# Turning k and q on VectorE instead of TensorE in an attention-and-MLP kernel, with another split of the weight conversion and another fixed order

## The chip, the cores and the metric

The kernel runs on one core of a Trainium2 chip. A core has a matmul engine (TensorE, PE in the profile, with its weight loads shown as PEld), a vector engine (VectorE, DVE), an activation engine (ScalarE, ACT), a general engine (GpSimd, POOL) and a queue engine that issues most transfers (SyncE, SP). Each engine works through its own list of instructions in order and waits on semaphores for the others. The metric is device time in microseconds (us) of one execution; lower is better.

## The reference

Two blocks follow each other. The first is attention with random features (8 batches, 8 heads, 576 positions, 64 values a head, 128 features); the second takes the result as a matrix of 8 x 576 rows of 512, adds the real part of its two-dimensional Fourier transform, and applies a normalised two-layer MLP with 2048 hidden values.

```python
q_s, k_s = q * scale, k * scale
def phi(x):                                   # x: b h s d
    proj = einsum('bhsd,md->bhsm', x, omega)
    h = proj - sum(x * x, -1) / 2
    return exp(h - max(h, -1)) / sqrt(m)
q_p, k_p = phi(q_s), phi(k_s)
kv  = einsum('bhsm,bhsd->bhmd', k_p, v);  z = sum(k_p, axis=2)
out = (q_p @ kv) / (q_p @ z + 1e-06)
x   = out.transpose(0, 2, 1, 3).reshape(8, 576, 512)
u   = x + real(fft(fft(x, axis=1), axis=2))
un  = (u - mean(u)) / sqrt(var(u) + 1e-06)
y   = u + maximum(un @ w_ch1, 0) @ w_ch2
```

q, k, v and omega come as float32, the two weight matrices as float64.

## The kernel before

The work has two parts.

**The first part** holds the attention, the Fourier mixing, the conversion of the weights to float32, the MLP of the first 512 rows ("plain"), and preparations for the second part. Attention goes over 32 pairs of heads (`attn(n)`, L573), three pairs in flight. For a pair, the 128 partitions hold 64 blocks of nine positions for each of two heads, so k and q are nine slices of 128 x 64 each.

1. `loads` (L369) brings k and q of a pair into one buffer `kq` with one transfer each (L376, L379) on SP; there are two such buffers. `load_v` (L381) brings v (L384).
2. `transposed` (L495) turns k and q on PE: nine 128 x 128 transposes against an identity (L512), each of them two slices. They land in PSUM, and `evicted` (L516) copies them to `kqT` on ACT or DVE (L526, L528).
3. `pairs_of` (L592) multiplies the turned slices by omega (L606), in three groups of 4, 1 and 4 transposes. The first six pairs use matmuls with 64 x 128 weights ("wide"), the others four quarter-sized ones.
4. `softmax` (L542) takes the maximum over the features on DVE (L549) and the exponential on ACT (L566), 18 exponentials of 128 x 128 a pair.
5. The features of k are multiplied with v (L640); `keep` (L649) copies the sums to `kv` on DVE or ACT (L654, L656).
6. The features of q are turned on PE, again nine transposes and three evictions, which also bring the positions into the order of the Fourier step (`qeT`).
7. Numerator and denominator (L687, L695), then the division on DVE (L704, L705, L716) or with ACT (L712).

`mix` (L728) does the Fourier step for a batch after its four pairs: sums and differences ("folds", L743 to L779, DVE or POOL), matmuls against tables (L799 to L860), combinations (L898, L901 on DVE) and sums into x (L910, L911, DVE or POOL), which go to memory as `us`.

`narrow` (L427) turns a 128 x 512 piece of float64 weights into float32, 32 pieces in all, each brought by one 512 KB transfer (L469) into one of four `slab` buffers. A step on ACT or POOL scales the high words (L439, L437); DVE takes the sign bit (L442), shifts the bits and joins the sign (L444), masks the exponent (L447) and scales the low words by it (L449); a last add, on POOL or DVE, joins both (L455). When all are converted, `w2_parts` (L1119) forms sums of the second weights (L1138, DVE or POOL) in the slabs and stores them (L1161, L1163), and `block_norms` (L1097) prepares the first block of the second part (norms L966, factors L1113).

**The second part** (from L1252) does the MLP of the other rows in eight blocks of 512 with products of sums; weights come back from memory through 13 `wl` buffers (L1335). `weight_sums` (L1183) makes the sums of the first weights, the first quarter of them in a tile of its own.

**The order.** All steps are generators that yield a `Step`: the engine (or a choice of engines), an estimated duration, what it waits for, what buffers and PSUM banks it takes and gives. `Listing.run` (L184) keeps a clock per engine and picks one step after the other; the order in which it picks them is the order of every engine's list. In the first part a string `PICKS` (L63) fixes each choice, one character for a step: which waiting stream goes on, and whether its second-best engine is taken. The banks are chosen by the clock. The second part has no string and goes by the clock and a bias in each step. SP's transfers stand in the same order, and one that waits for a buffer holds back all behind it.

Of the kernel before, what the change touches and what calls it, by code (L numbers as in the profile page):

```python
# [39 lines left out]
class Clock(NamedTuple):  # L40
# [16 lines left out]
DIGITS = "0123456789abcdefghijklmnopqrstuvwxyzABCDEFGHIJKLMNOPQRSTUVWXYZ!#$%&()*+,"  # L57
# [4 lines left out]

PICKS = (  # L63
    "40e0f03eafdaegebg3NbcbeefdcOdeccfgdb37ghj0gjj7hlP79Kj7ik97i8S7efhjffeHldfPiehdjfdOShgihidaKOdbRhciff"
    "ecgOfeejdfdPdeeedgSfdffdOfd8Kiii88jhd8jP8b99i8e8jcddghjgheiifcecdciieicgPgdef9cdghbkededfgchbggb79ij"
    "8hi7hjaPN97aj9gfffeg8eif8hcej1jccc7ehidbhffLiQObfbeG766gggfcbjahj9Ofghhjj8dgkkgT6jghff8de6dUjfhbgegh"
    "MefRafjUf8jgciSjeckkhjakkaeikggjlioklnRSgodonON7l7l6nnj9icadc97cibPJIej788a7edhclhkmjjagVijihkkfpVim"
    "oklilTTillaghlhnmVjkmpjkhhnmkimlgglmbjpjjg9d9alafhhdjlacdTback0j766k7lh4g89Gck6gkki77gij5ijhgj6dimni"
    "3ndjgi6Kc4jldlaikbkaijbhf75dcjlmUVUDGci45jciekajkkUk5kihoUeaeobaiodlenMSdonbiiljjcWjjkboijjkkhgMfkik"
    "hiflkmOFF99nol5m8jT7naabda89Rbj97ecdl8cjilegiPkQb4acahg57ebbgabgdjkdTkk6eceebb5f9dg4RGce486ggg6egfhh"  # L70
    "fg4g9egf5cbdRgfhhhcgjhggejigibbmHnbedijj6Neb7biihi9bgihckaffPa8cijdhbdghbaeibdefffacjiciQSfi9JJ75ih5"
    "jgjI699ajfg6g7fgefd65bO6Kalkkgd5jgjikagfldliPJpeoaeeOPQNejadgilgicljiSSFe65k56kl5Hk7j67S9lilk9gliih6"
    "ffUgec4fg4dbgg7fedaif5gfbheefilddddddeQhg9kbfncggRcfkkafkag6ngb65p5Hopoj4bhoaXbelli68bjjl5b7dlhiQRhi"
    "lflhpkgiWomjknmmmUimnjbjhnJjkm5akPFgedccff6Wf7idUVhi8Th3fogbqp8fgmkeidjna7ckeXYghmnmffnjeo79q6547oa4"
    "nlkpd7aceonnc8bViVicilbhmjim8fh7Snn8l5mkkPjgfRhfhihg8ghfbS4kjf83j4lllb79jei8mnUblfnmmiolpilOki9Mh5l5"
    "pmnaOm79jjVmkbblekFiji9a9kffjgjikhiihfgjafhgfigh4g50fff0ba5fdh9dghda77hgfdcbg8eO988jcehefibjjkellPcc"
    "fcdhgcihPgcffba2f82b3c98cbcdcd6a299efgddb9KGQQbefLa9ecf74gg9867RgP9idg8kgOhePP7be6ff2e5cc8fbMgdaf8f8"
# [44 lines left out]
class Listing:  # L122
# [4 lines left out]
    def __init__(self, buffers):  # L127
# [4 lines left out]
        self.moved = 0.0  # L132
        self.mode = "whole"
        self.banks = [0.0] * 8
        self.got = None

    def banks_at(self, n, t):

# [142 lines left out]
def kernel(  # L281
# [29 lines left out]

    NS = 3
    NV = 3
    NKQ = 2
    NE = 7
    NWIDE = 6

# [1252 lines left out]
```

## Time and profile before

| | |
|---|---|
| median of 3 runs | 1179.16 us (1177.43 to 1181.72) |
| span of the profiled execution | 1180.9 us |
| first part, up to the first matmul of L1252 | 423.7 us |
| second part | 757.3 us |
| busy over the span: PE, DVE, ACT, POOL | 1164.9, 722.6, 452.4, 412.9 us |
| busy in the first part: PE, DVE, ACT, POOL | 412.7, 340.8, 282.3, 174.5 us |
| transfers in the first part | 181 GB/s, share of the 16 transfer engines 0.60 |

The profile gives the span of its own execution, which is within the spread of the timed runs; a separate time of that execution is not listed. A line of groups reads: source line, engine, operation, output <- input, shapes, count | busy us, mean ns | idle time of the engine ahead of it and who ended it. The chain is the work that ended last, followed back step by step. Matmuls are pipelined and their durations overlap, so PE's busy time says less than the chain's pieces, in which each matmul is counted from the end of the one before.

### The profile page before, as it was taken

To read this page: it belongs to the slowest core of one execution; us is meant where nothing else is said; L and a number is where in the kernel's file an instruction comes from. 1 tells how busy PE (TensorE), PEld (TensorE's weight loads), DVE (VectorE), ACT (ScalarE), POOL (GpSimd) and SP (SyncE) were. 2 spreads that over 40 slices of the span, in tenths; PEclk is the share of its full clock that TensorE was granted. 3 is DMA by queue.
4 is the path that set the end of the run, shared out by engine and by line. 5 is a ranking of instruction groups with operands and counts; after the bars stand their busy time and mean duration, and the time that the engine had idled before them with its cause. 6 is when DMAs were issued, how large, how long until landed. Compare 5 with 4: busy or idle time off the path is not lost.

```text
span 1180.9 us, 31428 instructions
## 1 busy us (share of the span) xinstructions
PE 1164.9 (99%) x12549; PEld 1044.6 (88%) x12549; DVE 722.6 (61%) x1552; ACT 452.4 (38%) x1513; POOL 412.9 (35%) x489
## 2 busy tenths in 40 slices
PE   8999999999999999999999999999999999999998
PEld 7878888779787878998998998998999899899898
DVE  7989999976677642762662572473374275266255
ACT  7987888866343212222222222222222222222211
POOL 2443544455462124214314304223322421431421
PEclk9999999999999999999999999999999999999999
DMA  8855756666662260861771582384295095177155
GB/s 238 245 165 173 244 174 180 200 197 178 188 203 91 88 224 10 291 194 52 240 242 64 174 286 85 118 293 134 63 304 179 10 301 193 44 245 236 63 169 189
DMA packets 144705, 205.67 MB, mean 174 GB/s; under 512 B 49072, under 2 KB 58544, under 8 KB 144560
## 3 DMA queue, kind: packets, MB, share of 16 engines
q1 hardware_dynamic: 144064, 203.41, 53.9%
q8 instruction: 99, 1.62, 0.6%
q14 instruction: 46, 0.38, 0.1%
q10 hardware_dynamic: 496, 0.26, 0.1%
HBM read 171.90 MB, written 35.91 MB: 176 GB/s over the span
## 4 chain that ended last, share of the span: by engine, by line
PE 90%; DVE 4%; DMA 3%; ACT 1%; issue 1%; SPq 1%; DVEq 0%; ACTq 0%
PE banks L1252 33%; PE banks L1432 30%; PE banks L1045 5%; PE banks L606 4%; PE banks L1068 4%; PE banks L512 4%; PE banks L640 2%; PE banks L687 2%; DMA kq<-in_q_dram 2%; PE banks L985 2%; PE banks L849 1%; PE banks L799 1%; DVE nmx L549 1%; PE banks L809 1%; DMA kq<-in_k_dram 1%
## 5 line engine op out<-in xcount | busy, mean ns | idle before, releaser
L1238 DVE CUSTOM_DVE_ANT_0 hid<-banks,s 128x256 f32<-128x256 f32 x192 | 79.6, 423 | 255.4 <-PE banks L1252 250.5
L1432 PE MATMUL banks<-wl,sums 128*128 128x128 f32 x1792 | 217.3, 275 | 0.0
L1432 PEld LDWEIGHTS banks<-wl,sums 128*128 128x128 f32 x1792 | 208.8, 192 | 0.4
L566 ACT ACTIVATE e<-banks,nmx 128x128 f32<-128x128 f32 x576 | 164.7, 428 | 24.5 <-DVE nmx L549 24.0
L1266 ACT ACTIVATE s<-banks 128x256 f32<-128x256 f32 x192 | 73.7, 384 | 261.1 <-PE banks L1252 261.1
L1252 PE MATMUL banks<-unT,w 128*128 128x256 f32 x704 | 167.5, 379 | 0.0
L1252 PEld LDWEIGHTS banks<-unT,w 128*128 128x128 f32 x704 | 132.7, 190 | 17.9 <-issue 0.5
L1407 ACT ACTIVATE s<-banks 128x128 f32<-128x128 f32 x168 | 46.6, 278 | 242.3 <-PE banks L1432 195.7
L1252 PE MATMUL banks<-tt,w1s 128*128 128x256 f32 x512 | 126.2, 379 | 0.0
L1319 POOL TENSOR_TENSOR hs<-hid 128x256 f32<-128x256 f32 x64 | 46.4, 725 | 207.9 <-DVE hid L1238 178.9
L1252 PEld LDWEIGHTS banks<-tt,w1s 128*128 128x128 f32 x512 | 97.3, 190 | 13.2
L1412 DVE TENSOR_TENSOR part<-banks,s 128x128 f32<-128x128 f32 x168 | 48.8, 291 | 88.6 <-PE banks L1432 88.4
L549 DVE TENSOR_REDUCE nmx<-banks 128x8 f32<-128x1024 f32 (+1 forms) x96 | 89.3, 951 | 21.6 <-PE banks L606 16.8
L1432 PE MATMUL banks<-wl,hid 128*128 128x128 f32 x768 | 97.6, 275 | 0.0
L1432 PEld LDWEIGHTS banks<-wl,hid 128*128 128x128 f32 x768 | 93.5, 192 | 1.2
L1319 POOL TENSOR_TENSOR hs<-hid,hs 128x256 f32<-128x256 f32 x64 | 46.6, 728 | 119.8 <-issue 94.9
L606 PE MATMUL banks<-om,kqT 64*64 64x128 f32 (+1 forms) x2088 | 80.2, 278 | 2.2 <-ACT kv L656 0.9
L1252 PE MATMUL banks<-unT,w1s 128*128 128x256 f32 x320 | 80.7, 379 | 0.0
L606 PEld LDWEIGHTS banks<-om,kqT 64*64 64x64 f32 (+1 forms) x2088 | 65.4, 140 | 13.8 <-issue 4.4
L979 POOL TENSOR_TENSOR rstd<-rstd,mhalf 128x1 f32<-128x1 f32 x36 | 24.8, 689 | 149.6 <-DVE rstd L977 148.6
L1432 PE MATMUL banks<-wl,hs 128*128 128x128 f32 x576 | 74.9, 275 | 0.4 <-DVE part L1412 0.4
L1432 PEld LDWEIGHTS banks<-wl,hs 128*128 128x128 f32 x576 | 70.0, 192 | 0.9 <-DVE part L1412 0.6
(128 smaller groups left out, 1951.6 us busy)
## 6 DMA issues: line engine op xcount, KB each, us to landing
wl<-w2l SPq DMA_DIRECT2D x392, 256.0 KB, 3.6
raw<-in_moe_w_ch_dram SPq DMA_DIRECT2D x32, 512.0 KB, 5.0
kq<-in_k_dram SPq DMA_DIRECT2D x32, 288.0 KB, 4.4
kq<-in_q_dram SPq DMA_DIRECT2D x32, 288.0 KB, 4.8
vd<-in_v_dram SPq DMA_DIRECT2D x32, 288.0 KB, 4.9
u<-us SPq DMA_DIRECT2D x36, 256.0 KB, 3.9
ur<-us SPq DMA_DIRECT2D x36, 256.0 KB, 3.8
out_dram<-ur SPq DMA_DIRECT2D x34, 256.0 KB, 2.4
```

The lines of the kernel that those rows point to most:

```text
L512: nc.tensor.transpose(ps[:, (j - j0) * 128 : (j - j0 + 1) * 128], src(j), ident[:])
L549: nc.vector.tensor_reduce(nmx[:, :, 0:num], pps[:, :, 0 : MF * num].rearrange("p b (c m) -> p b c m", m=MF), axis=AX.X, op=ALU.max, negate ...
L566: nc.scalar.activation(out=e[:, c + (i if num == 1 else 0), :], in_=pps[:, i, MF * c : MF * c + MF], func=AF.Exp, bias=nmx[:, i, c : c + 1],)
L606: nc.tensor.matmul(pps[cols, c, MF * m : MF * m + MF], lhsT=kqT[rows, j, cols], rhs=om2[rows, :],)
L1045: nc.tensor.matmul(hp[:, 0:TP], lhsT=w1[:, dc, 128 * fc : 128 * fc + 128], rhs=unTs[key][:, dc, :], start=(dc == 0), stop=(dc == NDC - 1),)
L1068: nc.tensor.matmul(yp[:, 0:DM], lhsT=hs[fc][:, 128 * i : 128 * i + 128], rhs=w2[:, fc, :], start=(fc == 0), stop=(fc == NFC - 1),)
L1238: nc.vector._custom_dve(TENSOR_ADD_SAT, out=o, in0=ps, in1=sb, s0=FMAX, s1=0.0)
L1252: nc.tensor.matmul(ps[:, 0:HT], lhsT=left(dc), rhs=right(dc), start=start and dc == 0, stop=(dc == D2 - 1), skip_group_check=True,)
L1266: nc.scalar.activation(out=s[:], in_=ps[:, 0:HT], func=AF.Copy)
L1319: nc.gpsimd.tensor_tensor(out=o, in0=l, in1=r, op=op)
L1412: nc.vector.tensor_tensor(out=part[:, t, 128 * m : 128 * m + 128], in0=ps[:, 0:128], in1=saved[with_][:], op=ALU.add,)
L1432: nc.tensor.matmul(ps[:, 0:128], lhsT=left[:, f], rhs=wls[j, i, n][:, f], start=start and f == 0, stop=(f == 3), skip_group_check=True,)
```

## The change

**k and q.** Each of them is brought separately into a buffer `kq` of 128 partitions x 1120 values; three buffers. For each of the two heads, 32 rows of 18 positions are loaded twice, into two groups of 32 partitions, the second time 32 values later ("shifted"). In a row of the buffer every second run of 32 values then belongs to one half of the head's 64 values, so that a DVE transpose of 32 x 32 blocks, over the runs at even places, gives a tile whose partitions are the 64 values of each head and whose columns are the positions. For k this is one instruction of 576 values, written at every second place; for q it is one of 512 and one of 64. The PE transposes of k and q and their evictions are gone. All projections are quarter-sized. The positions are grouped otherwise than before, so v is loaded in four pieces to match, the product with v keeps two partial sums, and `keep` adds them with a DVE reduction. The features of q take ten transposes (2, 4 and 4) instead of nine.

**The weights.** ACT scales the low words by a power of two and converts them (32 passes more); the two DVE passes over the exponent and the low words are gone; the last add is always on POOL.

**The sums of w2** and their stores: each store is its own step, and the next sums wait for the stores that read their tile only.

**Buffers.** `wl` has 12 instead of 13; the sums of the first weights for the first quarter, and part of those for the second, go into three `kq` buffers, so `kq` stays allocated in the second part.

**The order.** `PICKS` has two characters for a step: the stream, and the engine with the bank. On SP the last of the 32 weight transfers stands after the loads of 30 pairs (before: 25), the first part has 548 transfers (before: 260), and over the first part folds, sums into x and sums of w2 change between DVE and POOL: 24 sums of w2 go from POOL to DVE, and 16 of the last fold steps (L772), 6 of the first (L743) and 6 pairs of sums into x (L910, L911) go the other way, each net.

```diff
-    NKQ = 2
+    NKQ = 3
+    NTURN = 3
+    NQE = 2
-    NWIDE = 6
+    XR = 2 * R * D - D // 2
-    NWL, NSUM = 13, 3
+    NWL, NSUM = 12, 3
...
     def loads():
-            yield Step(SP, 0.37, 3.0, take=("kq",), makes=("k", n), kb=288)
-            kq = ld.tile([P, 2 * R, D], F32, name="kq", tag="kq")
-            nc.sync.dma_start(kq[:, 0:R, :], k[b, h].rearrange(rows, r=R))
-            yield Step(SP, 0.47, 3.6, makes=("kq", n), kb=288, bias=-2.98)
-            nc.sync.dma_start(kq[:, R : 2 * R, :], q[b, h].rearrange(rows, r=R))
+            for name, src in (("k", k), ("q", q)):
+                yield Step(SP, 1.35, 3.0, take=("kq",), makes=(name, n), kb=560, ...)
+                t = ld.tile([P, XR], F32, name="kq", tag="kq")
+                for i in range(2):
+                    rows = src[b, 2 * pr + i].rearrange("(x r) d -> x (r d)", r=2 * R)
+                    for dh in range(2):
+                        p0 = D * i + 32 * dh
+                        nc.sync.dma_start(t[p0 : p0 + 32, :], rows[:, 32 * dh : 32 * dh + XR])
...
     def load_v(n):
+        for i, h, r0, r1, c0 in ((0, 0, 0, 5, 0), (0, 1, 5, 9, 0), (1, 0, 0, 4, 5), (1, 1, 4, 9, 4)):
+            nc.sync.dma_start(vds[n % NV][D * h : D * h + D, c0 : c0 + r1 - r0, 0:D], ...)
...
     def narrow(i, dst, raw):
+        def rounding():
+            yield Step(ACT, 0.57, after=(("raw", i),), makes=("low", i), bias=1.11)
+            nc.scalar.activation(out=lo, in_=lo, func=AF.Copy, scale=2.0**-29)
+        yield Fork(rounding())
...
-        nc.vector.tensor_scalar(sign[:], bits, 0xFF800000, None, op0=ALU.bitwise_and)
-        nc.vector.scalar_tensor_tensor(
-            lof, lo, 2.0**-52, sign[:].bitcast(F32), op0=ALU.mult, op1=ALU.mult
-        )
-        step = Step({POOL: 1.25, DVE: 0.61}, makes=("w", i), give=("slab",), ...)
-        eng.tensor_tensor(out=dst, in0=dst, in1=lof, op=ALU.add)
+        yield Step(POOL, 1.25, after=(("low", i),), makes=("w", i), give=("slab",), ...)
+        nc.gpsimd.tensor_tensor(out=bits, in0=bits, in1=lo, op=ALU.add)
...
+    def turn(name, n):
+        yield Step(DVE, 0.7, after=((name, n),), take=("kT",), give=("kq",), makes=(name + "T", n))
+        t = att.tile([128, 2 * R * 32], F32, name="kT", tag="kT", bufs=NTURN)
+        raw = kqs.pop((name, n))[:].rearrange("p (r d) -> p r d", d=32)[:, ::2, :]
+        raw = raw.rearrange("p (s c) y -> p s c y", s=2)
+        if name == "k":
+            nc.vector.transpose(t[:].rearrange("p (c x s) -> p s c x", c=R, s=2), raw)
+        else:
+            nc.vector.transpose(
+                t[:, 0 : 64 * (R - 1)].rearrange("p (s x w) -> p s w x", s=2, x=32), raw[:, :, R - 1 : 0 : -1]
+            )
+            nc.vector.transpose(t[:, 64 * (R - 1) :].rearrange("p (s x) -> p s x", s=2), raw[:, :, 0])
+        return t
...
     def attn(n):
-        kqT = yield from transposed(...)
+        kT = yield from turn("k", n)
+        def turn_q():
+            qTs.append((yield from turn("q", n)))
+        yield Fork(turn_q())
...
+        yield from projected(lambda i, h, m: of_k(i, (NC + 1) * h + m), NC, 0, 1, after=(("kT", n), "om2"))
+        yield from projected(
+            lambda i, h, m: of_k(i, NC) if i == h else first_of_q(i), 1, 2, after=(("qT", n),), give=("kT",)
+        )
+        yield from projected(lambda i, h, m: of_q(i, m, h), NC, 3, 4, give=("kT",))
...
         def keep():
-            step = Step({DVE: 0.2, ACT: 0.16}, take=("kv",), give=(kvb,), makes=("kv", n))
+            yield Step(DVE, 0.34, take=("kv",), give=(kvb,), makes=("kv", n))
+            nc.vector.tensor_reduce(
+                kv[:]..., kvp[:, :, 0:n2].rearrange("m h d -> m d h"), axis=AX.X, op=ALU.add
+            )
...
     def w2_parts():
-            yield Step(SP, 3.0, 4.0, after=(("w2t", i),), kb=7 * 256, makes=("w2l", i))
             for n, t in ((0, c11), (1, c21), (4, c22)):
+                yield Step(SP, 0.6, 2.6, kb=256, makes=("w2l", i, n))
                 nc.sync.dma_start(w2l[i][n].rearrange("p (f m) -> p f m", f=4), t)
             for n, t in ((2, sums[0]), (5, sums[1])):
+                yield Step(SP, 0.6, 3.4, kb=512, makes=("w2l", i, n))
...
+            of_big = stored[0:3] if part is summed else of_big
+            of_sums = stored[3:5]
```

## The prediction

> **What bounds the kernel now.** I read the stretches first, then the chain that ended last, then the groups by line. The stretches (us, then busy us of PE, weight loads, DVE, ACT and POOL, then PE clock, DMA share, GB/s) are the first part up to 200, its rest, and the second part, which begins when line L1252 starts:
>
> ```profile
> 0.00:200.00 200.00, 191.00 (x4042) 164.91 (x4044) 178.86 (x382) 170.64 (x609) 77.07 (x79) 0.99 0.69 204
> 200.00:423.70 223.70, 221.72 (x3470) 176.68 (x3471) 161.94 (x369) 111.68 (x398) 97.41 (x101) 1.00 0.52 160
> 423.70:1181.00 757.30, 752.13 (x5041) 703.03 (x5039) 381.84 (x802) 170.07 (x507) 238.40 (x309) 1.00 0.52 170
> ```
>
> The reader should see that PE looks full everywhere, but that until 200 us DVE is 89% and ACT 85% busy as well, and the loads are at 204 GB/s. The change leaves the second part's matmuls alone, so its 757 us stay. In the chain, the pieces of the first part give a price per matmul (start, us, what; an ordinary fp32 matmul has two records, a transpose one):
>
> ```profile
> 11.35 1.09 PE banks L606 x16
> 203.67 3.10 PE banks L512 x27
> 206.77 1.25 PE banks L606 x40
> 410.00 13.73 PE banks L1068 x32
> ```
>
> A transpose costs 3.10/27 = 0.115 us, a wide projection 1.09/8 = 0.136, a quarter one 1.25/20 = 0.0625. From 200 us on the chain is PE nearly throughout, at the end MLP matmuls at 13.73/32 a record that wait for nothing; before 200 it changes between DVE, DMA, ACT and PE. The groups that carry DVE's prices (count | busy us, mean ns | idle before):
>
> ```profile
> L549 DVE TENSOR_REDUCE nmx<-banks 128x8 f32<-128x1024 f32 x64 | 77.5, 1217 | 10.3 <-PE banks L606 8.3 <-ACT e L566 1.4 <-ACT qeT L528 0.2
> L444 DVE SCALAR_TENSOR_TENSOR w<-w,sign 128x512 uint32<-128x512 uint32 x32 | 23.4, 731 | 0.3
> L449 DVE SCALAR_TENSOR_TENSOR raw<-raw,sign 128x512 f32<-128x512 uint32 x32 | 22.0, 687 | 0.6
> L447 DVE TENSOR_SCALAR sign<-w 128x512 uint32<-128x512 uint32 x32 | 15.9, 496 | 1.1
> L749 DVE TENSOR_TENSOR half<-half 128x510 f32<-128x510 f32 x16 | 11.0, 685 | 0.0
> L526 DVE COPY kqT<-banks 128x512 f32<-128x512 f32 x15 | 10.3, 684 | 1.5 <-PE banks L512 1.5
> L749 DVE TENSOR_TENSOR half<-x 128x255 f32<-128x255 f32 x16 | 6.7, 416 | 0.0
> ```
>
> None but the first has an idle time ahead of it worth naming: DVE runs back to back.
>
> **The change, part by part.** *PE.* The 288 transposes of k and q go (33.1 us), 32 more of the features come (3.7), and the 108 wide projections of the first six pairs become 216 quarter ones (14.7 to 13.5). Net -30.6 us.
>
> *DVE.* It loses the kqT copies (15 x 0.684 + 12 x 0.285 = 13.7), 12 kv copies (3.4), L447 and L449 (37.9), four last adds of the narrowing (2.8), and to POOL a net 19.2 of the folds and of x (16 x 0.569, 6 x 1.339 and 6 x 1.033 less 2.5 and 1.6 that come back). It gains 24 sums of w2 from POOL (x 0.69 = 16.6), two divisions (1.6), a reduction of kv in every pair and the turns. The reduction reads 260 values; nearest is the 256-value maximum, 0.419: 32 x 0.42 = 13.4. No row shows a turn. One pair turns 576, 512 and 64 values. From the two L749 rows a plain pass costs 0.15 us + 1.055 ns a value: 0.755 + 0.687 + 0.215 = 1.66 us. Ends: at L447's 0.97 ns a value with nothing fixed 1.1, with L444's 0.731 for 512 and a 0.33 row for 64 about 1.9; I take 1.66 because a turn, like L749, is a plain pass over SBUF values. 32 x 1.66 = 53.0. Net about +6; neighbours overlap by 0.057 us (rows sum to 384 us, busy is 341, 750 instructions), so the engine's total goes from 352 to 356 in this count.
>
> On PE the rows put nine transposes and their evictions at 1.04 us of PE and about 1.3 of ACT or DVE a pair; the turn is 1.66 us of DVE alone. The Trainium skill speaks against that move: its page "VectorE: DVE Perf Modes", section "Rules for kernel authors", gives a 128x128 transpose to TensorE where PSUM is an acceptable destination; read as a price, the move gains nothing. Its page "Vector Engine (DVE) Microarchitecture Reference", section "The reshape front-end and per-opcode configuration", has the 32x32 turn run at one value per cycle: at that engine's 0.96 GHz an estimate of 1.2 us a pair, by which DVE's column below would be 15 us shorter and PE's would decide, 393. No row of this trace shows a turn.
>
> A turn waits for its four loads at its place in DVE's list. Queued behind it are the maxima of other pairs, for which ACT's exponentials wait; what a late load costs there is priced under the rivals. The wait of nine transposes on PE for the same loads (4.4 us in the idle time of that group) goes.
>
> *ACT* loses 35.6 (kqT), 6.6 (kv) and 6.8 (x); it gains 32 rounding passes (0.784 as in the same-sized L439: 25.1) and about 11.7 of qeT copies: net about -12 of 282. *POOL* gains folds, x and four adds and loses 24 sums of w2 (1.3 each): net about +7 of 174, hidden by its idle 58%. POOL's last add now waits for ACT's rounding; queued behind it are folds and x sums, and for those the mixing matmuls wait. Bounds 0 to 32 x 0.78 = 25 us if each delay went through; I take 0, since both ACT passes start from the same landed load and DVE's two passes (0.556 + 0.731) lie ahead of the add anyway.
>
> *Loads.* Each k or q is four transfers of 32 rows x 4480 B, v four instead of one. The first part's issues on SP go from 260 to 548; at the 0.33 to 0.43 us of L376 and L379 that is +109 us of SP time. Its cover is SP's waiting: 41.0 us in L469 for POOL and 40.3 in L376 for PE, among 250 in all. Bytes go from 76.9 to 94.8 MB. At 302 GB/s per full share (181 at 0.60) that is 314 us of transfer time in 400. Buffers: three single tiles, freed by the turn, in place of two double ones freed by PE. Every transfer also waits until the eighth before it has landed, as before; eight of 143 KB make 1.1 MB in flight.
>
> The page "DMA: Bandwidth & Descriptors", section "Rules for kernel authors", speaks against this: use 128 partitions and at least 1 MiB per transfer, and don't split into partition groups. Its fit of 2.0 us + bytes/436 GB/s would make 2.3 us of each, so eight in flight would still ask for 490 GB/s: an estimate by which the split itself costs nothing. The trace has 2.6 us for its 128 KB stores and no load of this size.
>
> *Start.* The first projection ran at 6.24 us. Now four issues of about 0.4 us, the same 3.2 us to landing and a turn of 0.76 give about 6.1: nothing, ends -1 and +2. *Second part.* 12 wl buffers for 13: twelve leaves of 0.895 us cover a landing of 3.6 us; six sums go to DVE, half idle there: nothing, ends -1 and +2.
>
> **The sum.** I go down each engine's list in the order in which its instructions stand and add the prices. Columns: normalisation (L704) number; before: DVE, PE, when it really ran; after: DVE, PE.
>
> - 20th: 193, 180, ran 209.6; after 181, 162
> - 24th: 245, 242, ran 273.0; after 216, 193
> - 28th: 273, 281, ran 312.5; after 256, 225
> - 32nd: 316, 344, ran 378.5; after 308, 293
> - end: 352, 388, ended 423.6; after 356, 357
>
> Before, the time is the larger column plus 17 to 36 us. After, DVE leads until the 32nd: 308 + 34 = 342. PE has 64 us left then, of which some can be no earlier: end at 406. If PE's own column decides, 357 + 36 = 393. A third path checks it: the weights stand later among the loads (the last of 32 after 30 pairs, before after 25), so w2's sums end later, at 331 in DVE's new column, which with 31 us over it is 362. Before, POOL did the last of them at 371.5 and the first block's factors (L1113) were ready at 415.5, 44 us later by way of the stores, the norms and their loads; the same 44 make 406, and less if the stores, now waited for one by one, come free earlier. I take the middle, 400: -24 us. The profiled span, 1180.9, becomes 1157; it stands 1.7 above the median of the runs, 1179.2, so the forecast for the median is 1155. The likeliest case's own range: at the low end PE's 393, 1148; at the high end 406 and 8 us of dearer turns (32 x 0.24), 1169.
>
> **Rivals.** *DVE decides against it.* If a turn is worse than every row suggests, DVE's column carries it one to one. At 2.2 us a pair the gain is gone (18 us of 32 turns); at twice my price (3.3) the 32nd comes at 395 and the end near 459, 1214. For it: DVE is back to back and no row has a cross-partition move. Against: 2.2 is above the dearest streaming row.
>
> *The loads fall behind (slower).* With the 30th pair's q, 70.2 MB must be in, against 58.8 before, when that load was issued at 295 us (199 GB/s). That load comes some 100 us before the end (26 us of DVE to the 32nd, 10 from landing to normalisation, 64 of PE), so the forecast needs 70.2 MB in 300 us, 234 GB/s. At 217 GB/s it is no faster; at the 204 of the first 200 us it ends at 444, 1200. For it: the chain has DMA pieces of 6.5 us already. Against: the share is 0.69, and 236 GB/s were held in the first 50 us.
>
> *PE's relief comes whole.* DVE's turns are at their low end (32 x -0.56, 406 - 18 = 388), and over PE's column only the 28 us of the 24th normalisation, 357 + 28 = 385: -31 to -39, 1140 to 1148. For it: the last adds and both bit passes leave the engine that was full until 250 us. *No change:* the stretch after 200, with 12 of 32 pairs, is PE-bound, and 12 x 0.96 us is an 11 us floor there, so an exact balance is unlikely.
>
> **How the numbers follow.** Forecast case 0.50, whole relief 0.16, a part of the gain lost to loads or DVE (1169 to 1175) 0.11, no change 0.05, slower by loads 0.12, slower by DVE 0.06. Within 0.3% (3.5 us), about what a measurement can tell from no change, is 1175.6 to 1182.7. So faster 0.77, same 0.05, slower 0.18. The range leaves 0.05 below 1139 and some 0.15 above 1184.
>
> **What would show it.** Right: no kqT in any group, L1252 starting at 393 to 406, transposes on DVE of 0.7 to 0.8 us, DVE over 85% busy until the 32nd normalisation, DMA near 230 GB/s up to 300 us. Wrong: turns over 1 us; PE waiting on DVE turns behind loads of k and q; SP's longest waits being for its own earlier transfers; a gap ahead of L1252 because that third path ends last (before, it had 8 us to spare).

## The result, and the profile after

The changed kernel takes 1226.1 us (median of 4 runs, 1221.0 to 1231.1); the kernel before took 1180.4 beside it. The ratio is 1.039, with a 95% interval of 1.036 to 1.042: slower by 46 us, where the prediction said 24 us faster. The profiled execution has a span of 1224.3 us. These are its stretches, with the columns of the table shown of before (us, busy us of PE, weight loads, DVE, ACT and POOL, PE clock, DMA share, GB/s); the second part begins with line L1288, at 461.8 us:

```profile
0.00:200.00 200.00, 163.75 (x3611) 140.95 (x3611) 154.13 (x317) 131.11 (x448) 79.12 (x88) 0.92 0.86 215
200.00:461.80 261.80, 242.89 (x3861) 189.71 (x3860) 206.15 (x437) 132.92 (x459) 101.68 (x106) 0.98 0.69 200
461.80:1224.30 762.50, 752.80 (x5041) 702.68 (x5039) 378.17 (x803) 170.84 (x507) 236.71 (x309) 1.00 0.52 168
```

The first part grew from 423.7 to 461.8 us, the second from 757.3 to 762.5. Up to 200 us no engine is full any more: PE fell from 191 to 164 us busy, DVE from 179 to 154, ACT from 171 to 131. What is fuller is the transfers: their share went from 0.69 to 0.86, but the rate only from 204 to 215 GB/s. A full share is now worth 250 GB/s (215/0.86), where it was worth 296. The granted clock of PE in this stretch is 0.92, before 0.99.

The chain that ended last says the same. Up to 200 us its transfers add up to 76 us and its matmuls to 29; before it was 29 us of transfers, single ones of up to 6.75 us among them, and 101 of matmuls. These are some of its long pieces (start, us, what; most lie between the ones shown):

```profile
14.60 5.17 DMA kq<-in_k_dram
27.11 4.84 DMA kq<-in_q_dram
45.68 5.18 DMA kq<-in_q_dram
155.75 5.07 DMA kq<-in_q_dram
193.05 8.05 DMA raw<-in_moe_w_ch_dram
251.23 5.54 DMA kq<-in_k_dram
396.29 13.60 PE banks L1069 x120
```

Up to 260 us the chain returns again and again to a landing of k, q or weights; only the end of the first part is PE without a wait, as before. The groups of DVE (count | busy us, mean ns | idle before it and who ended that):

```profile
L588 DVE TENSOR_REDUCE nmx<-banks 128x8 f32<-128x1024 f32 (+1 forms) x96 | 88.2, 944 | 7.4 <-PE banks L643 7.4
L535 DVE STREAM_TRANSPOSE kT<-kq 128x512 f32<-128x512 f32 x32 | 35.5, 1109 | 27.4 <-DMA kq<-in_q_dram 27.4
L479 DVE SCALAR_TENSOR_TENSOR w<-w,sign 128x512 uint32<-128x512 uint32 x32 | 28.4, 888 | 2.6 <-DVE sign L477 0.5
L532 DVE STREAM_TRANSPOSE kT<-kq 128x576 f32<-128x576 f32 x32 | 24.7, 773 | 6.1 <-DMA kq<-in_k_dram 5.8 <-DMA kq<-in_q_dram 0.2
L691 DVE TENSOR_REDUCE kv<-banks 128x130 f32<-128x260 f32 x32 | 13.3, 414 | 8.5 <-PE banks L678 8.3
L538 DVE STREAM_TRANSPOSE kT<-kq 128x64 f32<-128x64 f32 x32 | 6.7, 209 | 0.0
```

Two prices differ from the prediction's: the turn of q (1.109 us instead of 0.687) and the pass that joins the sign (0.888 instead of 0.731). And the turns have idle time ahead of them that transfers end. Behind a waiting turn stand the maxima, and behind those the exponentials; from the list of waits (us in total, times, longest; the last line is SP's own):

```profile
ACT e L605 <- DVE nmx L588: 72.9, 44, 8.4
DVE kT L535 <- DMA kq<-in_q_dram: 27.4, 16, 3.7
SPq L403 <- DMA raw<-in_moe_w_ch_dram: 27.7, 17, 4.4
```

Before, ACT waited 24.0 us for maxima, and SP's longest waits were for POOL and PE. Now SP waits much less for engines (42 us up to 350 us, before 180), and its longest wait, the last line, is for the landing of its own earlier transfers: 49 us of such waits up to 350 us, before 22. Summed over its records up to 350 us, SP spends 262 us issuing transfers, before 148.

### The profile page after: what moved, and what is told of

Read it like the earlier page. It is cut to its first block, busy times and chain, and to the rows that moved or that the text cites. A ratio compares the mean times of both kernels' runs of the same rounds, so it can differ in the third digit from the quotient of the medians.

```text
span 1224.3 us, 31767 instructions
## 1 busy us (share of the span) xinstructions
PE 1159.4 (95%) x12509; PEld 1033.3 (84%) x12509; DVE 738.4 (60%) x1556; ACT 434.9 (36%) x1414; POOL 417.5 (34%) x502
## 4 chain that ended last, share of the span: by engine, by line
PE 78%; DMA 8%; DVE 6%; issue 3%; SPq 2%; ACT 1%; POOL 1%; DVEq 0%; ACTq 0%; POOLq 0%
PE banks L1288 32%; PE banks L1468 28%; PE banks L1092 5%; PE banks L1069 4%; DMA kq<-in_q_dram 3%; PE banks L643 2%; DMA raw<-in_moe_w_ch_dram 2%; DMA kq<-in_k_dram 2%; SPq L403 1%; DVE nmx L588 1%; PE banks L711 1%; PE banks L555 1%; PE banks L678 1%; PE banks L1009 1%; PE banks L823 1%
## 5 line engine op out<-in xcount | busy, mean ns | idle before, releaser
L605 ACT ACTIVATE e<-banks,nmx 128x128 f32<-128x128 f32 x576 | 157.8, 398 | 78.4 <-DVE nmx L588 72.9
L1288 PE MATMUL banks<-unT,w 128*128 128x256 f32 x704 | 166.3, 379 | 0.0
L1288 PEld LDWEIGHTS banks<-unT,w 128*128 128x128 f32 x704 | 133.2, 190 | 18.3 <-issue 0.5
L1288 PE MATMUL banks<-tt,w1s 128*128 128x256 f32 x512 | 127.4, 379 | 0.0
L643 PE MATMUL banks<-om,kT 64*64 64x128 f32 x2304 | 88.0, 285 | 26.0 <-DVE kT L538 8.4
L1288 PEld LDWEIGHTS banks<-tt,w1s 128*128 128x128 f32 x512 | 97.2, 190 | 13.5 <-DVE ur L1105 0.3
L643 PEld LDWEIGHTS banks<-om,kT 64*64 64x64 f32 x2304 | 69.4, 139 | 40.9 <-DVE kT L538 10.8
L1288 PE MATMUL banks<-unT,w1s 128*128 128x256 f32 x320 | 79.5, 379 | 0.0
L1288 PEld LDWEIGHTS banks<-unT,w1s 128*128 128x128 f32 x320 | 60.4, 190 | 8.7
```

The lines of the kernel that those rows point to most:

```text
L605: nc.scalar.activation(out=e[:, c + (i if num == 1 else 0), :], in_=pps[:, i, MF * c : MF * c + MF], func=AF.Exp, bias=nmx[:, i, c : c + 1],)
L643: nc.tensor.matmul(pps[D * h : D * h + D, i, MF * m : MF * m + MF], lhsT=left(i, h, m), rhs=om2[D * i : D * i + D, :],)
L1288: nc.tensor.matmul(ps[:, 0:HT], lhsT=left(dc), rhs=right(dc), start=start and dc == 0, stop=(dc == D2 - 1), skip_group_check=True,)
```

## The experiments

Two theories stood at the start. *Loads*: the new form of the loads costs all of the loss and more. *Order and DVE*: the dearer turns and the new order cost it, and the landings in the chain only look like causes. Times are medians; each run has its own interval of the ratio to the kernel before. "First part" is the start of the second part in the profile: 423.6 us before, 461.8 in the changed kernel. It is that of the one profiled execution, which can stand some 3 us off the median of its kernel.

**k and q loaded only once.**

```diff
+                if n:
+                    kqs[name, n] = kqs[name, 0]
+                    continue
```

> The changed kernel, but k and q are loaded for the first pair alone and every later pair turns that same tile, so 504 of the 512 transfers of k and q are left out (36 MB); all turns, matmuls, v, weights and the order stay. The output is therefore not the reference's. Loads theory (the transfers of k and q hold the first part up, as issue time or as transfer time): the order then runs as my columns had it, L1252 at 393 to 406 us and 1150 to 1165 us. DVE theory (the q turn at 1.11 us instead of 0.69 and the last reads of DVE decide): DVE's work is unchanged, so L1252 stays above 440 us and the time above 1205 us.

Measured: 1178.9 us, ratio 1.000 (0.999 to 1.001), first part 414.2. Neither number came. The loads of k and q cost 47 us (461.8 to 414.2 in the first part). But without them the change is still no faster than the kernel before. Here DVE is as full as the prediction thought:

```profile
0.00:200.00 200.00, 179.99 (x4323) 156.76 (x4327) 180.00 (x381) 156.15 (x538) 96.95 (x109) 0.98 0.51 137
200.00:414.20 214.20, 207.33 (x3155) 160.43 (x3148) 178.01 (x375) 106.19 (x370) 83.88 (x85) 1.00 0.49 152
```

So there were two questions: what in the loads costs 47 us, and where the other half of the forecast's gain went.

**v in one transfer, as before** (96 issues fewer; the positions of v are not those that the turned k needs, so the numbers are of other data).

```diff
-        for i, h, r0, r1, c0 in ((0, 0, 0, 5, 0), (0, 1, 5, 9, 0), (1, 0, 0, 4, 5), (1, 1, 4, 9, 4)):
-            nc.sync.dma_start(
-                vds[n % NV][D * h : D * h + D, c0 : c0 + r1 - r0, 0:D],
-                v[b, 2 * pr + i].rearrange("(p r) d -> p r d", r=R)[:, r0:r1, :],
-            )
+        nc.sync.dma_start(vds[n % NV][:, :, 0:D], v[b, 2 * pr : 2 * pr + 2].rearrange("i (p r) d -> (i p) r d", r=R))
```

> The changed kernel with v loaded by one transfer per pair as before (96 fewer issues on SP, same bytes and same 256 B rows); the slices of v then meet the wrong positions, so the output is not the reference's. Issue theory (SP's issuing is the limit): 128 issues at 0.61 us become 32, some 58 us of SP's time go, and the first part falls by 15 to 40 us, 1185 to 1211 us. Transfer theory (the 16 engines are the limit): their work is the same, so within 5 us of 1226.

Measured: 1206.1 us, ratio 1.023 (1.021 to 1.025): 20 us less than the changed kernel, with the same bytes. The number of issues matters, or their form.

**k and q in one transfer each of 128 partitions** (rows of the same 4480 bytes from other places, 192 issues fewer).

```diff
-                for i in range(2):
-                    rows = src[b, 2 * pr + i].rearrange("(x r) d -> x (r d)", r=2 * R)
-                    for dh in range(2):
-                        p0 = D * i + 32 * dh
-                        nc.sync.dma_start(t[p0 : p0 + 32, :], rows[:, 32 * dh : 32 * dh + XR])
+                nc.sync.dma_start(t[:], bass.AP(tensor=src.tensor, offset=src.offset + at, ap=[[step, P], [1, XR]]))
```

> The changed kernel with each k or q brought by one transfer of 128 rows x 4480 B (rows 2176 B apart, so they overlap in memory and are not the right rows: output not the reference's). Bytes and row length are the same, issues on SP fall by 192. Issue theory: some 80 us of SP's time go, 1175 to 1200 us, with rows still at about 281 ns. Transfer theory, because of the groups of 32 partitions: the rows fall to 180 to 210 ns each and the time to 1170 to 1195 us. Transfer theory, because of the bytes alone: rows stay at 281 ns and the time stays above 1215 us.

Measured: 1198.1 us (four runs from 1186.9 to 1200.8), ratio 1.013 (1.008 to 1.018), first part 436.4: 28 us less. By the trace's records of single rows, a row of 4480 bytes takes a transfer engine 217 ns here and 281 ns in the changed kernel. The four groups cost issues, and they seem to make each row dearer too. The rows overlap in memory here, which may have a part in it; the split of the kernel before (below), with its own rows, shows a smaller step, 115 to 128 ns.

**Both at once.**

> The changed kernel with both edits at once: k and q in one transfer of 128 partitions x 4480 bytes each and v in one, as it had been (the rows are not the right ones, so the numbers are of other data). Issues on SP as in the kernel before, bytes as in the changed one (94.8 MB). If issues and groups of 32 partitions make the loads dear, this takes back nearly all of the 47 us that the loads cost: 1179 to 1186, SP issuing for some 160 to 170 us of the first 350. If the extra bytes have a part of their own, at least the 10 us stay that they cost in the kernel before: 1189 to 1196.

Measured: 1197.3 us, ratio 1.015 (1.014 to 1.017), first part 432.9; SP issues for 136 us of the first 350. The gains don't add: in the first part the two edits bring 21.9 and 25.4 us alone and 28.9 together. The run with k and q loaded once has v in four pieces, so the one to hold beside it is that with k and q in one transfer each, which has them too: of the 47.6 us of k and q, 25.4 go to the number and form of their transfers, and 22.2 stay (436.4 - 414.2; by the medians 28.0 and 19.2). What stays is all that is left of loading k and q, 36 MB in 64 transfers. How much of it the added 17.8 MB make is not shown; in the kernel before they cost at most 10 us (below).

**Half of the transfers on ACT's queue** (those of a pair's second head).

```diff
+                        eng = nc.scalar if i else nc.sync
-                        nc.sync.dma_start(t[p0 : p0 + 32, :], rows[:, 32 * dh : 32 * dh + XR])
+                        eng.dma_start(t[p0 : p0 + 32, :], rows[:, 32 * dh : 32 * dh + XR])
```

> The changed kernel with the second head's two transfers of every k and q issued by ACT instead of SP: 128 issues (about 54 us at 0.42) move, nothing else. Issue theory: 10 to 30 us faster than the changed kernel, 1196 to 1216 us, less what ACT's waits for a free buffer cost. Transfer theory: no faster than 1220 us, and slower where ACT's exponentials queue behind a transfer that waits.

Measured: 1262.4 us, ratio 1.071 (1.069 to 1.073). This speaks neither for nor against SP's share in the loss. ACT spends 56 us on 128 issues, in a list written without them, and stands still for 26 us ahead of them, nearly all of it until an earlier transfer has landed. The program has eight semaphores for landings, SP and ACT share them, and none is used again before its transfer has landed: SP, with 192 us of issues in the first 350, waits 91 us for such landings instead of 49.

**The kernel before, with split loads, with more bytes, and with small extra transfers.** These put one part of the new loads each into the old order: first the split (k shown, q alike), then the other two, of which each run has one.

```diff
-            nc.sync.dma_start(kq[:, 0:R, :], k[b, h].rearrange(rows, r=R))
+            for p0 in range(0, P, 32):
+                nc.sync.dma_start(kq[p0 : p0 + 32, 0:R, :], k[b, h].rearrange(rows, r=R)[p0 : p0 + 32])
```

```diff
+            nc.sync.dma_start(spare[:, at : at + 544], rows[:, 0:544])    # bytes: 128 x 2176 bytes more
+        for p0 in (0, 32, 64):                                            # small: three of 1 KB more
+            nc.sync.dma_start(spare[p0 : p0 + 32, at : at + 8], rows[p0 : p0 + 32, 0:8])
```

In the second one the extra bytes fall on a quarter of the first weights, so its output is of other weights.

> The kernel before with each load of k and of q as four transfers of 32 partitions instead of one of 128: the same bytes to the same places, 192 more issues on SP (64 loads become 256). If it is the number of transfers and their 32 partitions that made the loads of the changed kernel dear, the 2304-byte rows take clearly more than the 115 ns they took before (the 4480-byte ones took 281 in groups of 32 and 217 in one transfer of 128 partitions), the stretches up to 200 us show a DMA share near 0.85 for the same GB/s or fewer, and the time rises by 10 to 30 us: 1190 to 1210. If the extra 17.8 MB are what counts, the split alone is hidden: 1177 to 1185, rows at 115 to 130 ns.

> The kernel before with one more transfer after each load of k and of q, 128 partitions of 2176 bytes of the same tensor into a tile that the first part does not read: 17.8 MB more, as in the changed kernel, by 64 issues of the cheap form. If the bytes are what counts, the stretches up to 300 us go to 240 GB/s or more and k and q come late: 1190 to 1215. If the number of transfers and their groups of 32 partitions count, the bytes are hidden (before, the share up to 200 us was 0.69): 1178 to 1186.

> The kernel before with three more transfers after each load of k and of q, each of 32 partitions x 32 bytes (1 KB, 0.2 MB in all) into columns of a tile that the first part does not read (the weights there are overwritten, so the output is of other weights): 192 more issues on SP, no bytes to speak of, and the loads themselves whole. If the time of SP's issues sets the loss (SP issues for 147 of the first 350 us before, for 229 with every load split, which took 1205), this one takes as long as the split: 1198 to 1208. If the groups of 32 partitions are slow by their data, the small ones cost nothing: 1178 to 1184.

Measured: split 1204.9 us (1.021, 1.020 to 1.023), bytes 1189.4 (1.009, 1.007 to 1.010), small ones 1199.9 (1.018, 1.015 to 1.020). First the stretch up to 200 us with the extra bytes, then the one with the small transfers:

```profile
0.00:200.00 200.00, 186.88 (x3926) 161.20 (x3927) 172.52 (x367) 164.63 (x588) 75.94 (x78) 0.99 0.83 254
```

```profile
0.00:200.00 200.00, 179.38 (x3751) 155.04 (x3753) 163.49 (x347) 157.33 (x562) 72.49 (x75) 0.97 0.65 187
```

17.8 MB more at 254 GB/s cost 10 us. This is the most that can be put down to the bytes, since they come by 64 issues more (187 us of SP's first 350, before 148). 192 transfers of nearly nothing cost 21 us, while the transfer engines have more room than before (0.65 of their time, before 0.69). In that run SP's issues take 234 us of the first 350 and stand ahead of the loads that matter; in the chain of the first part SP's issuing has 27 us, before 7. A rival is that the eight places in flight run out. SP's waits for earlier landings up to 350 us are 26 us here and 22 before, so the 21 us are SP's time in the main. In the changed kernel these waits are 49 us, and no run separates the 27 us more from the issues. The split takes 5 us longer than the small transfers, and its rows take 128 instead of 115 ns.

**Two transfers of 64 partitions for four of 32** (the changed kernel, its own data).

```diff
+                    ap = [[32, 2], [2 * R * D, 32], [1, XR]]
+                    nc.sync.dma_start(t[D * i : D * i + D, :], bass.AP(tensor=src.tensor, offset=src.offset + at, ap=ap))
```

> The changed kernel with its own data, and each load of k and of q as two transfers of 64 partitions (one for a head, the two feature halves in one pattern) instead of four of 32: 128 issues on SP fewer. One transfer of 128 took 28 us off for 192 issues fewer; by issues this is 2/3 of it: 1204 to 1212. If the group of 32 is what a row's price hangs on, and 64 are free of it, the 4480-byte rows fall from 281 to near 217 ns and all of the 28 us come: 1196 to 1202.

Measured: 1759.3 us, ratio 1.492. Both expectations missed by far. The stretch shows why:

```profile
0.00:200.00 200.00, 75.06 (x1379) 65.57 (x1379) 56.09 (x110) 50.65 (x175) 20.14 (x30) 0.73 0.24 77
```

77 GB/s: by the records of rows, for 689 of the first 990 us exactly two rows of k or q were in flight; the changed kernel has 13 or more in flight for half of the time that it has any. The outermost step of the pattern counts two, which fits two transfer engines doing the work. The Trainium skill states it: "DMA: Bandwidth & Descriptors", section "Rules for kernel authors", lets an outermost dimension of size c below 16 confine a transfer to at most c engines. The run says nothing on the number of issues, which it was made for.

**q's turn with another order of writing** (k and q loaded once; the positions stand in another order, so the numbers are of other positions).

```diff
-                t[:, 0 : 64 * (R - 1)].rearrange("p (s x w) -> p s w x", s=2, x=32), raw[:, :, R - 1 : 0 : -1]
+                t[:, 0 : 64 * (R - 1)].rearrange("p (s w x) -> p s w x", s=2, x=32), raw[:, :, R - 1 : 0 : -1]
```

> The changed kernel with k and q loaded once only (as in the run that took 1179) and with q's turn writing its 32-position blocks one after another instead of every ninth place, so that the positions stand in another order and the numbers are of other positions; the same instructions on every engine. If DVE's column is what is left once the loads are cheap (93 to 97% busy from 50 to 300 us there), the turn of q falls from 1.10 us to 0.69 to 0.77 and 32 x 0.33 to 0.41 us come off the end: 1165 to 1170. If the turn's write order does not set its price it stays near 1.1 us and the time at 1179. If the price falls and the time does not, the order of the steps, not DVE's column, sets the first part's end: 1176 to 1180.

Measured: 1175.9 us, ratio 0.997 (0.996 to 0.999), first part 409.1. The group of the turn in this run:

```profile
L538 DVE STREAM_TRANSPOSE kT<-kq 128x512 f32<-128x512 f32 x32 | 21.9, 685 | 1.5 <-DMA kq<-in_q_dram 1.5
```

The turn falls from 1102 to 685 ns, which is the prediction's 0.687, so the price hangs on where the values are written. Of the 13.4 us of DVE time that this frees, the first part gets 5.1 in the profiled executions; the medians differ by 3.0.

**The sums of the second part on their old engines** (on top of the run before).

```diff
-            step = Step({POOL: 1.35, DVE: 0.7}, port=True, **kw, bias=0.06)
+            step = Step({POOL: 1.35} if pool else {DVE: 0.7}, port=True, **kw, bias=0.06)     # pool: i in (1, 2, 4)
```

> As the run before it, and the sums of the second part on the engines that they had in the kernel before: of the eleven of a block, those of the products 1, 2 and 4 on POOL and all others on DVE, where the change has the second one of 4, the first of 5 and one of 7 on POOL. If that choice is what makes a block of the second part 95.05 us instead of 94.28 (DVE sums a S-combination late once a block in the chain), 4 to 6 us go: the second part back at 757 us, the whole 1160 to 1166. If the twelfth weight buffer instead of the thirteenth is the cause, the second part stays at 762 and the time is that of the run before it within 1 us.

Measured: 1183.6 us, ratio 1.005 (1.003 to 1.007): 8 us slower, where one theory wanted 5 faster and the other no change. Both fall. What costs time shows in each block of the second part of the changed kernel, here in the form that five of the seven have (start, us, engine, line, operation):

```profile
619.15 0.72 POOL L1355 TENSOR_TENSOR hid<-hid 128x256 f32<-128x256 f32 x1
619.18 0.97 DVE L1005 TENSOR_SCALAR u<-u,mv,rstd 128x512 f32<-128x512 f32 x1
619.83 0.91 POOL L1355 TENSOR_TENSOR hs<-hid,hs 128x256 f32<-128x256 f32 x1
620.08 1.21 DVE L1435 TENSOR_TENSOR sums<-hid,sums 128x512 f32<-128x512 f32 x1
621.21 0.53 DVE L1005 TENSOR_SCALAR u<-u,mv,rstd 128x512 f32<-128x512 f32 x1
621.80 0.66 PE L1009 MATMUL banks<-ident,u 128*128 128x128 f32 x4 [0.64 <-DVE u L1005]
```

The first normalisation (L1005) takes 0.97 us beside a POOL sum and the second, alone, 0.53; the sum between them takes 1.21 instead of 0.68. PE stands still for the second normalisation, 4.5 us over seven blocks, nearly all of the 5.2 that the second part lost. (In the other two blocks the second normalisation lies beside a sum.) The kernel before had a stretched pass there too, 1.50 us in each block, but PE's weight loads waited only 1.6 us for it in all: what is new is where the passes fall. In the run with the sums moved, two 1.27 us POOL sums fall beside the two normalisations, which take up to 1.52 us; PE waits 9.5 us for them instead of 4.5, and the second part is 10 us longer again; the other 5 us were not traced. The page "SBUF — State Buffer", section "SBUF: two separate sides", describes an exclusive lock on a port pair that VectorE and GpSimd share, held for a whole instruction. The durations here point the same way: 0.54 us alone and 1.52 beside a sum of 1.27 that started 0.03 earlier, 0.26 less than one after the other.

**The new narrowing alone, in the kernel before**: the rounding pass on ACT beside the first step, two DVE passes out, all adds on POOL; then the same with ACT's pass later, just ahead of the add.

```diff
+        nc.scalar.activation(out=lo, in_=lo, func=AF.Copy, scale=2.0**-29)
-        nc.vector.tensor_scalar(sign[:], bits, 0xFF800000, None, op0=ALU.bitwise_and)
-        nc.vector.scalar_tensor_tensor(lof, lo, 2.0**-52, sign[:].bitcast(F32), op0=ALU.mult, op1=ALU.mult)
-        eng.tensor_tensor(out=dst, in0=dst, in1=lof, op=ALU.add)
+        nc.gpsimd.tensor_tensor(out=bits, in0=bits, in1=lo, op=ALU.add)
```

> The kernel before with the change's narrowing of the weights alone: one rounding pass of 0.57 to 0.78 us on ACT for each of the 32 pieces instead of two DVE passes of 0.496 and 0.687, and the last add always on POOL as an integer add; the order of everything else as it was. By the prediction's terms DVE loses 40 us and ACT gains 25, in the stretch where DVE is 89 and ACT 85% busy; if DVE's column sets that stretch, 8 to 20 us come off: 1159 to 1171. If ACT, now first in the stretch, takes the place, or DVE's passes beside POOL's adds stretch as in the changed kernel (681 to 2351 ns) : 1175 to 1184.

> The kernel before with the change's narrowing alone once more, the rounding pass on ACT put later in the list: where the second of the two dropped DVE passes stood, just ahead of the add, instead of beside the first pass. If the 25 us that the narrowing alone cost came from ACT standing still for a piece of weights that had not landed (exponentials behind it), they go, and what DVE's 40 us are worth is seen: 1160 to 1176. If they come from ACT's 25 us of work and from all adds on POOL, the place changes little: 1195 to 1206.

Measured: 1204.7 us (1.021, 1.020 to 1.022) and 1195.8 (1.014, 1.012 to 1.016). The place is worth 9 us, and 16 stay. In the later form POOL's adds wait 82.3 us for ACT's pass in all, not much longer than they waited for DVE before (77.9). What such a wait holds up shows in a piece of the chain of the later form (start, us, what):

```profile
70.82 5.37 issue
76.23 1.28 POOL w L451
77.51 0.69 POOL x L906
78.20 0.60 POOL x L907
78.82 0.59 SPq L921
...
80.13 4.63 DMA raw<-in_moe_w_ch_dram
...
85.35 0.64 ACT raw L448
85.99 0.83 ACT qeT L524 x3
86.86 2.05 PE banks L683 x32
```

The chain has 5.37 us as "issue" ahead of POOL's add. The list of POOL's instructions names what it stood for, ACT's rounding pass (start, us, what, idle time before it):

```profile
76.22 1.29 POOL L451 TENSOR_TENSOR w<-w,raw 128x512 uint32<-128x512 uint32 x1 [5.39 <-ACT raw L448]
```

POOL stands at the add, the sums of x (L906, L907) stand behind it, SP's store of x (L921) waits for these, the next weights stand behind the store, and ACT waits for the weights with copies queued behind that PE needs: PE waits 8.4 us at the end of this piece.

**Its parts**: the two DVE passes left out with nothing in their place, and the same with ACT's pass added, its result not used.

```diff
-        nc.vector.tensor_scalar(sign[:], bits, 0xFF800000, None, op0=ALU.bitwise_and)
-        nc.vector.scalar_tensor_tensor(lof, lo, 2.0**-52, sign[:].bitcast(F32), op0=ALU.mult, op1=ALU.mult)
+        nc.scalar.activation(out=lo, in_=lo, func=AF.Copy, scale=2.0**-29)       # second run only
```

> The kernel before without the two DVE passes of the narrowing that the change drops (the bit pass, 32 x 0.496, and the scaling, 32 x 0.687), and nothing in their place; the last add adds the high part to itself, so the low parts are left out and the weights are twice as large. This measures the largest term of the forecast by itself. If DVE's column sets the first 250 us, 38 us less of it bring 10 to 25 us: 1154 to 1169. If the written order, made for the old durations, leaves DVE to wait for the other engines instead, less than a third of it comes: 1170 to 1180.

> The kernel before without the two DVE passes, as in the run that took 1179.8, and with the rounding pass on ACT at the late place, its result not used (the add stays on the engines it had, POOL for most and DVE for a few, and adds the high part to itself, so the low parts are left out). If ACT's 25 us of passes are what made the narrowing cost 15 to 25 us, by holding up the exponentials and evictions behind them on a list that is 85% busy: 1190 to 1198. If it is the wait of POOL's add for ACT, and the sums queued behind that add: 1178 to 1184.

Measured: 1179.8 us (1.000, 0.999 to 1.002) and 1183.4 (1.003, 1.002 to 1.004). 38 us less of DVE bring nothing in the old order; its profile has DVE at 156 us of the first 200 instead of 179, and PE at 191 as before:

```profile
0.00:200.00 200.00, 191.47 (x4180) 166.46 (x4184) 156.41 (x344) 172.77 (x620) 76.47 (x85) 1.00 0.70 210
```

25 us more on ACT cost 3 to 4 us. So of the 16 us of the later form, about 12 (1195.8 less 1183.4) come with POOL's adds: their wait for ACT, with what is queued behind them, and the four that went from DVE to POOL. No run separates these two; the chain shows the first.

## Why the prediction was wrong

The first part divides as follows. With k and q loaded once and q's turn at its forecast price it ends at 409.1, against a forecast of 400; the price of the turn makes it 414.2, the loads 461.8. The second part adds 5.2.

**The loads are the step that failed**, 47.6 us priced at nothing. "+109 us of SP time" was right in size (148 to 262 us up to 350 us). "Its cover is SP's waiting" was not: a sum of waits says that SP is free at times, not that it is free ahead of the load that is needed next. 192 tiny transfers, hidden by the same argument, cost 21 us. "At 302 GB/s per full share" took the rate of the old transfers for the new ones, which got 250 up to 200 us: 281 ns a row of 4480 bytes in groups of 32 partitions, 217 in one transfer. The rule against partition groups that the prediction quoted from the page "DMA: Bandwidth & Descriptors" was right for this case; the estimate drawn from its fit, that the split costs nothing, was not, as it holds no price for an issue and none for a row. The page has that fit for transfers issued on GpSimd, and these are issued on SP.

**The rival "the loads fall behind" was the right mechanism**, given 0.12 and too small a loss. It asked for 234 GB/s up to the 30th pair's q for the forecast, and said that 217 would be no faster. Measured: 71.6 MB had moved when that turn started, at 331.4 us, so 216 GB/s. Its error is "100 us before the end". From the 30th turn to the end it took 130 us, in the changed kernel and in the two runs with loads taken out alike: not 36 but 66 us to the 32nd normalisation, then the 64 of PE that were forecast. With 130 us, breaking even (423.6) needs 70.2 MB in 294 us, 239 GB/s, and the forecast 260, more than the 236 of the fastest 50 us of before and than the 254 of the run with more bytes. Worked through, the rival would have been the forecast. Three of the signs named for being wrong came: turns over 1 us, PE waiting for turns (11.4 us ahead of L643), and SP's longest wait being for its own earlier transfers.

**DVE.** The turns of 576 and 64 values came as priced (0.773 and 0.209 us, forecast 0.755 and 0.215), the sum of kv too (0.414, forecast 0.42). The turn of q was mis-sized: 1.109 for 0.687, and with it the pair, 2.09 us, lies outside the bounds of 1.1 to 1.9. That is 13.4 us of DVE and 3 to 5 of the end. (DVE's net, "about +6", adds up to +7.6 from the terms listed; nothing hangs on it.) The joining pass is 5 us dearer in all: eight of its 32 take 1.03 to 2.35 us, each of them beside a POOL sum. The page "Vector Engine (DVE) Microarchitecture Reference", section "The reshape front-end and per-opcode configuration", gives one value per cycle; at the page's 0.96 GHz that is an estimate of 1.04 ns. With the other writing order q's turns agree, (685 - 203)/448 = 1.08 ns a value between the 512 and the 64; as written they take (1109 - 209)/448 = 2.01.

**The columns.** With the loads out and the turn cheap, the 20th, 24th, 28th and 32nd normalisations ran at 199.9, 237.3, 280.1 and 345.4 us. DVE's column had 181, 216, 256 and 308, so the distance is 19 to 37 us, where 17 to 36 was assumed, and the forecast for the last, 342, was 3 us off. The end by DVE was forecast at 406 and came at 409.1; taking the middle between two paths, 400, was the wrong choice. Counting down an engine's list held in that run; what it left out was whether its inputs arrive. That DVE's 38 us are worth nothing in the old order agrees too: there PE's column is the larger at the 28th and 32nd.

**The narrowing.** "I take 0" of 0 to 25 us for POOL's add waiting for ACT. It named what is queued behind, folds and x sums, but neither SP's store nor the loads behind that. In the old order, which was not made for it, the adds cost about 12 us; in the changed kernel POOL waits only 7.5 us for ACT's rounding. The runs in the old order don't show what the new order pays, and the 3 us between 406 and 409.1 leave little room.

**The second part**: "six sums go to DVE, half idle: nothing" was wrong by 5.2 us. The idle time is there, but a DVE pass that PE waits for came to lie beside a POOL sum. **The start** came 0.66 us later (6.90, forecast 6.1 and bounds to +2). **PE's relief** came: with loads out and the turn cheap, PE is busy for 385.7 us of the first part instead of 412.7: 27 us less, where 30.6 were forecast.

No version tried here beats both kernels by more than 0.3%. The only one clear of the kernel before (1175.9) loads k and q only once.

## What to carry to other kernels

Price a load by what it makes the issuing queue do, not by its bytes alone: splitting transfers takes the queue's time ahead of the load that is waited for, and a sum of the queue's waits is no cover. Before moving work between engines, work out by which time the last input must be in, and compare the rate this needs with the best rate that the profile shows. A gain on an engine is worth something only while its inputs keep up, and a relief of the second-fullest engine may be worth nothing.

## What the runs showed of the hardware

- An issue on SP took 0.42 us (median) for 32 partitions, with 140 KB as with 1 KB, 0.38 to 0.39 for one of 128 with 560 KB, and 0.61 us for a quarter of v: 192 transfers of 1 KB took 95 us of SP.
- Rows of 4480 bytes took a transfer engine 281 ns in transfers of 32 partitions and 217 in one of 128, from other places; with rows of 2304 bytes from the same places it was 128 and 115.
- With a pattern whose outermost step counts two, two rows of k or q were in flight for most of the time instead of 13 or more for half of it: 77 GB/s instead of 215.
- A 32x32 turn of 512 values took 0.685 us when it wrote the positions of a block one after another and 1.10 when it wrote to every eighth place (the expectation above says ninth).
- The DVE passes traced here lasted longer beside a POOL sum: the normalisation's 0.54 us became 0.97 to 1.52, a sum's 0.68 became 1.21, and the joining pass's 0.69 became 1.03 to 2.35.
- PE's granted clock fell where PE had gaps: 0.92 up to 200 us at 82% busy, 0.73 at 38% busy with two rows in flight, 0.99 at 96% before. What the lower clock itself cost was not measured.
